# Loading four units of V with two queues, 64 partitions each

## The chip, the cores and the metric

The kernel runs on one core of a Trainium2 chip. The metric is the device time of one execution in microseconds (us). Before the change it is 344.48 us, the median of 3 runs (344.44 to 344.49).

## The reference

One decode step for a batch of 2: an attention block over a cached K and V of 4096 positions and 32 heads, a small ReLU network, and a sigmoid gate that mixes the two.

```python
q = (x @ wq).reshape(B, Sq, Hq, Dh).transpose(0, 2, 1, 3)      # B 2, Sq 1, D 512, Hq 32, Dh 128
scores = jnp.einsum("bhqd,bhkd->bhqk", q, k) * (Dh ** -0.5)    # k, v: 2 x 32 x 4096 x 128, bf16
p = _softmax(scores, axis=-1)
o = jnp.einsum("bhqk,bhkd->bhqd", p, v)
a = o.transpose(0, 2, 1, 3).reshape(B, Sq, Hq * Dh) @ wo
b = relu(x @ w1) @ w2                                          # Dff 1376
g = _sigmoid((x * gate_w).sum(-1, keepdims=True))
return g * a + (1 - g) * b
```

K and V are 67.1 MB each. All inputs together are read once: 145.46 MB by the page.

## The kernel before

The kernel writes out the order of every engine by hand. A small class collects each engine's operations in a list; an operation names the marks it waits for (`waits`), the DMA counters it waits for (`dwaits`) and the mark it sets (`signal`). Each engine then runs its list in that order, so an operation that waits holds back all that stand behind it on its engine.

K and V are each cut into eight units, 0 to 7. A unit is eight heads of one batch entry: 32,768 rows of 128 numbers, 8.39 MB. `unit_in` views it as 128 partitions of 64 KB each, and a DMA of a whole unit writes all 128 partitions with one run of 65,536 bytes for each. The buffer `kv` has five slots of 32 KB per partition. `region` joins the first four in pairs into two places of 64 KB per partition, so that two whole units fit.

The program has three stages.

- Start (to about 20 us): x, the gate, wq and w1 come in, q is computed.
- K (to about 192 us): for each piece of K, VectorE transposes 32 by 32 blocks (line 384) and TensorE multiplies by q (line 405, and line 197 for its helper). Then the softmax (lines 410 to 431).
- V and the end. For unit u, `spread(u)` puts its softmax weights into the tile `ptm` (two copies on GpSimd, one on VectorE, one on ScalarE, lines 433 to 444). `v_unit(u)` runs 64 matmuls on TensorE over the unit's 64 KB (line 458); its first one waits for the unit's DMA counter, and the last one sets the mark `pe_v_u`. `v_extract(u)` masks and sums the result on VectorE (lines 464 and 468). `o_gather` collects the units, `project` applies wo, and `ffn_f` and `ffn_last` apply w2.

All large loads are issued by SyncE, whose list is also their queue (`q1` in the page, queue SP): w1, wq, ten K loads (line 269), then V. Unit u of V goes into place u % 2 of `region`, so its issue waits for `pe_v_(u-2)`, the end of the unit that lay there before. Units 0, 1, 3, 4, 5 and 6 are one DMA each (line 277). Unit 2 comes in two halves of 32 KB per partition, to slots 4 and 0 (line 274), and unit 7 in two halves to slots 2 and 3 (line 280), both issued after `pe_v_5`. Behind V stand wo (lines 282 and 283) and w2 (lines 284 and 288) on the same queue. The counters `sem_v` count landed DMAs, 16 for each, one from each of the 16 DMA engines.

ScalarE issues two small DMAs at the start (lines 262 and 263) and one at the end. In the V stage it has one copy per unit (line 444), which waits for `pe_v_(u-2)`.

Of the kernel before, what the change touches and what calls it, by code (L numbers as in the profile page):

```python
# [85 lines left out]
def bass_gated_mix__gqa_block_cached__dense_activation_relu__decode_kernel(  # L86
# [67 lines left out]
    def psf(p0, p1, c0, n):  # L154
        return PSF[p0:p1, c0:c0 + n]
# [18 lines left out]
    names = ["x", "gw", "wq", "w1", "wo0", "wo1", "w2a", "w2b", "w2c", "w2d", "w2e", "w2f", "out"]  # L174
    sem = {n: nc.alloc_semaphore("sem_" + n) for n in names}
    sem_k = [nc.alloc_semaphore(f"sem_k{s}") for s in range(3)]
    sem_v = [nc.alloc_semaphore(f"sem_v{s}") for s in range(3)]

    mk = {}
# [8 lines left out]
    def adder(engine):  # L188
        def add(fn, waits=(), signal=None, dwaits=()):
            P.add(engine, fn, waits=[marker(w) for w in waits], signal=marker(signal) if signal else None, dwaits=dwaits)  # L190
        return add

    pool, dve, act, pe, sp = (adder(e) for e in ("pool", "dve", "act", "pe", "sp"))
# [12 lines left out]
    def held_at(e, out, lhsT, rhs, g):  # L206
# [9 lines left out]
         waits=["c_i16z"], signal="c_i16")  # L216
# [5 lines left out]
         waits=["c_i32z"], signal="c_i32")  # L222
# [6 lines left out]
         waits=["c_s4z"], signal="c_s4")  # L229
# [7 lines left out]
    v_rows = A_v_cache.rearrange("b h s d -> (b h s) d")  # L237

    def unit_in(rows, u):
        return rows[u * 32768:(u + 1) * 32768, :].rearrange("(p r) d -> p (r d)", p=128)  # L240

    region = kv[:, 0:4, :].rearrange("p (g s) n -> p g (s n)", g=2)
# [23 lines left out]
    for g, (u, halves) in enumerate(segments):  # L266
# [3 lines left out]
           waits=([f"kt_{last_of[g - 3]}"] if g >= 3 else ["pe_qr1"] if g == 2 else []))  # L270
    for u in range(7):
        if u == 2:
            for hf, dst, w in ((0, kv[:, 4, :], "kt_63"), (1, kv[:, 0, :], "pe_v_0")):
                sp(lambda e, hf=hf, dst=dst: e.dma_start(dst, unit_in(v_rows, 2)[:, 16384 * hf:16384 * (hf + 1)]).then_inc(sem_v[2 - 2 * hf], 16),
                   waits=[w])
            continue
        sp(lambda e, u=u: e.dma_start(region[:, u % 2, :], unit_in(v_rows, u)).then_inc(sem_v[u % 2], 16),
           waits=([f"pe_v_{u - 2}"] if u >= 2 else [f"kt_{last_of[7]}"] if u == 0 else [f"kt_{last_of[8]}"]))
    for hf in range(2):
        sp(lambda e, hf=hf: e.dma_start(kv[:, 2 + hf, :], unit_in(v_rows, 7)[:, 16384 * hf:16384 * (hf + 1)]).then_inc(sem_v[1 + hf], 16),  # L280
           waits=(["pe_v_5"] if hf == 0 else []))
# [3 lines left out]
       waits=[f"pt_7_{hq}" for hq in range(4)])  # L285
# [147 lines left out]
    def spread(u):  # L433
        src = ET.rearrange("p (k f e) -> p f k e", f=16, e=2)
        for hq in range(4):
            args = dict(out=ptm[32 * hq:32 * hq + 32, u % 2, :, hq, :].rearrange("p (f k) e -> p f k e", f=2),
                        in_=src[32 * hq:32 * hq + 32, 2 * u:2 * u + 2])
            waits = ["dve_et3", "c_ptm"] + ([f"pe_v_{u - 2}"] if u >= 2 else [])
            if hq < 2:
                pool(lambda e, args=args: e.tensor_copy(**args), waits=waits, signal=f"pt_{u}_{hq}")  # L440
            elif hq == 2:
                dve(lambda e, args=args: e.tensor_copy(**args), waits=waits, signal=f"pt_{u}_{hq}")
            else:
                act(lambda e, args=args: e.activation(func=ACT.Copy, **args), waits=waits, signal=f"pt_{u}_{hq}")  # L444

    def v_unit(u):
        rows = region[:, u % 2, :].rearrange("p (m c d) -> p m c d", c=4, d=128)
        halves = [kv[:, s, :].rearrange("p (m c d) -> p m c d", c=4, d=128) for s in (4, 0)]
        for m in range(64):
            t = m % 4  # L450
            waits, dwaits = [], []
            if m == 0:
                waits = [f"pt_{u}_{hq}" for hq in range(4)] + ([f"dve_y{u - 2}"] if u >= 2 else [])
                dwaits = [(sem_v[2], 16) if u == 2 else (sem_v[u % 2], 16 * (u // 2 + 1))]
            if u in (2, 7) and m == 32:
                dwaits = [(sem_v[0], 32) if u == 2 else (sem_v[2], 32)]
            at = halves[m // 32][:, m % 32] if u == 2 else rows[:, m]
            pe(lambda e, m=m, t=t, at=at: e.matmul(  # L458
                psf(32 * t, 32 * t + 32, V_B[u % 2] * BANK, 512), lhsT=ptm[:, u % 2, 4 * m:4 * m + 4, :, :],
                rhs=at, start=(m < 4), stop=(m >= 60), tile_position=(0, 32 * t)),  # L460
               waits=waits, dwaits=dwaits, signal=(f"pe_v_{u}" if m == 63 else None))

    def v_extract(u):
        dve(lambda e: e.tensor_tensor(out=Y.rearrange("p (c d) -> p c d", c=4),  # L464
                                      in0=psf(0, 128, V_B[u % 2] * BANK, 512).rearrange("p (c d) -> p c d", c=4),
                                      in1=maskc[:, :].unsqueeze(2).to_broadcast([128, 4, 128]), op=ALU.mult),
            waits=[f"pe_v_{u}", "dve_maskc"] + ([f"dve_x{u - 1}"] if u else []), signal=f"dve_y{u}")
        dve(lambda e: e.tensor_reduce(out=X2[:, u, :], in_=Y.rearrange("p (c d) -> p d c", c=4), axis=AX.X, op=ALU.add),  # L468
            waits=[f"dve_y{u}"], signal=f"dve_x{u}")
# [10 lines left out]
    def o_gather(b, us):  # L480
        for u in us:
            pe(lambda e, u=u, b=b: e.matmul(psf(0, 32, O_C0, 128), lhsT=selx[:, 24 - 8 * u:56 - 8 * u], rhs=X2[:, 4 * b + u, :],
                                            start=(u == 0), stop=(u == 3)),
               waits=[f"dve_x{4 * b + u}"] + (["dve_rinv", "dve_selx"] if u == 0 else []) + (["dve_O0"] if b else []),
               signal=(f"pe_O{b}" if u == 3 else None))
        if 3 not in us:
            return
        dve(lambda v, b=b: v.tensor_scalar(out=O_sb[:, b, :], in0=psf(0, 32, O_C0, 128), scalar1=rinv[:, b:b + 1],
                                           scalar2=gb[0:32, b:b + 1], op0=ALU.mult, op1=ALU.mult),
            waits=[f"pe_O{b}", "dve_rinv", "dve_g"], signal=f"dve_O{b}")  # L490
        for dq in range(4):
            pe(lambda e, dq=dq, b=b: e.matmul(psf(0, 128, R_C0 + 32 * b, 32), lhsT=s4[:, dq, :], rhs=O_sb[:, b, 32 * dq:32 * dq + 32],
                                              start=(dq == 0), stop=(dq == 3), tile_position=(0, 0)),
               waits=([f"dve_O{b}", "c_s4"] if dq == 0 else []), signal=(f"pe_R{b}" if dq == 3 else None))
        dve(lambda v, b=b: v.tensor_copy(out=oW[:, :, b], in_=psf(0, 128, R_C0 + 32 * b, 32)), waits=[f"pe_R{b}"], signal=f"dve_oW{b}")
# [49 lines left out]
    for u in range(8):  # L545
        if u < 7:
            spread(u + 1)
        v_unit(u)
        v_extract(u)
        if u == 3:  # L550
            o_gather(0, [0, 1, 2])
        if u == 4:
            o_gather(0, [3])
# [46 lines left out]
```

## Time and profile before

| what | value |
|---|---|
| median of the runs | 344.48 us |
| the profiled execution's own time | 344.46 us |
| its span, first to last instruction | 343.2 us |
| mean granted TensorE clock | 0.806 |
| DMA rate over the span | 424 GB/s |
| TensorE matmul busy | 200.1 us (58%) |
| VectorE busy | 176.6 us (51%) |
| ScalarE busy | 22.8 us (7%) |
| GpSimd busy | 19.6 us (6%) |

The span leaves out 1.26 us of the execution's time before the first and after the last instruction. In the view of stretches, "(x)" counts instructions, PEclk is the granted TensorE clock and the DMA share is that of the core's 16 DMA engines. In the views of slices, a digit is the busy share in tenths, at most 9.

Where the trace lists each DMA packet, a run of 65,536 bytes into one partition is one packet; there are 1,536 of them, and 1,152 of 32,768 bytes.

When V's loads are issued and when TensorE starts on the unit, by the timeline:

| load | issued at, us | first matmul on it, us | unit's last matmul releases others at, us |
|---|---|---|---|
| unit 2, first half | 189.50 | 221.20 | |
| unit 2, second half | 209.24 | 230.81 | 234.46 |
| unit 3 | 216.78 | 250.27 | 256.64 |
| unit 4 | 234.46 | 269.61 | 274.85 |
| unit 5 | 256.64 | 288.98 | 294.77 |
| unit 6 | 274.85 | 308.31 | |
| unit 7, first half | 294.77 | 318.03 | |
| unit 7, second half | 295.1 | 327.65 | |

### The profile page before, as it was taken

The page shows a single profiled execution, that of the slowest core. Times are in us where ns is not written, and L with a number is a line of the kernel's source. Part 1 is how long each engine was busy: PE and PEld are TensorE (multiplying, and loading weights), DVE is VectorE, ACT ScalarE, POOL GpSimd, SP SyncE. Part 2 cuts the span into 40 slices and gives each one's busy share as a digit, 9 for nine tenths or more (in the row PEclk, how much of TensorE's full clock was granted, in tenths as well). Part 3 has the DMA queues.
Part 4 walks back from the last instruction along what each step waited for, and adds up shares of the span by engine and source line. Part 5 has one row for each costly group of instructions (what it writes and reads, how often), then busy time and mean ns, then how long its engine had stood idle before and what let it go on. Part 6 is the DMA issues. An engine that isn't in the chain of part 4 may idle for free.

```text
span 343.2 us, 2528 instructions
## 1 busy us (share of the span) xinstructions
PE 200.1 (58%) x1226; PEld 53.4 (16%) x970; DVE 176.6 (51%) x124; ACT 22.8 (7%) x70; POOL 19.6 (6%) x34
## 2 busy tenths in 40 slices
PE   0167429799969799699799337423080503306455
PEld 0141001111111111111111012200030201102121
DVE  2239059899789899698999562202001030201021
ACT  1040000000000000000000240000000000000000
POOL 8000000000000000000000041101000010100000
PEclk9985858999989999989999856865558575856568
DMA  8998989899998999998999989999999999899996
GB/s 348 428 489 369 481 374 481 378 477 428 422 489 367 429 443 466 392 466 382 475 428 428 468 382 424 441 466 413 443 413 445 435 420 474 384 420 443 428 400 236
DMA packets 4340, 145.61 MB, mean 424 GB/s; under 512 B 485, under 2 KB 1002, under 8 KB 1258
## 3 DMA queue, kind: packets, MB, share of 16 engines
q1 hardware_dynamic: 4322, 145.46, 98.5%
q8 instruction: 8, 0.13, 0.2%
q14 instruction: 2, 0.02, 0.0%
q10 hardware_dynamic: 8, 0.00, 0.0%
HBM read 145.46 MB, written 0.00 MB: 424 GB/s over the span
## 4 chain that ended last, share of the span: by engine, by line
DMA 67%; DVE 19%; PE 11%; ACT 1%; issue 1%; POOL 0%; SPq 0%; DVEq 0%
DMA kv<-in_A_k_cache_dram 31%; DMA kv<-in_A_v_cache_dram 19%; DVE kt L384 16%; DMA kt<-in_B_w_dram 12%; PE PS L458 7%; DMA kv<-in_A_wq_dram 4%; ACT kt L426 1%; PE PS L405 1%; PE PS L197 1%; PE PS L331 1%; DVE mpad L411 1%; DVE kt L468 1%; POOL ptm L440 0%; DVE qbuf L464 0%; DVE kt L430 0%
## 5 line engine op out<-in xcount | busy, mean ns | idle before, releaser
L384 DVE STREAM_TRANSPOSE kt<-kv 128x2048 f32<-128x2048 f32 x64 | 141.2, 2274 | 22.7 <-DMA kv<-in_A_k_cache_dram 22.7
L405 PE MATMUL PS<-kt,qbuf 128*128 128x512 bf16 x256 | 107.0, 418 | 30.4 <-DVE kt L384 25.3
L197 PE MATMUL PS<-kt,qbuf 128*128 128x512 bf16 x256 | 106.5, 416 | 0.0
L458 PE MATMUL PS<-kv,ptm 128*32 128x512 bf16 x512 | 48.7, 559 | 77.3 <-DMA kv<-in_A_v_cache_dram 73.8
L464 DVE TENSOR_TENSOR qbuf<-PS,maskc 128x512 f32<-128x512 f32 x8 | 5.5, 692 | 111.4 <-PE PS L458 111.4
L405 PEld LDWEIGHTS PS<-kt,qbuf 128*128 128x128 bf16 x256 | 25.8, 101 | 139.9 <-issue 71.4
L458 PEld LDWEIGHTS PS<-kv,ptm 128*32 128x32 bf16 x512 | 18.7, 131 | 106.0 <-issue 85.4
L440 POOL COPY ptm<-kt 32x512 bf16<-32x512 bf16 x16 | 11.2, 697 | 259.2 <-DVE rsum L472 175.9
L358 ACT ACTIVATE qbuf<-PS 32x8 bf16<-32x8 bf16 x40 | 7.8, 196 | 134.3 <-PE PS L197 133.0
L444 ACT ACTIVATE ptm<-kt 32x512 bf16<-32x512 bf16 x8 | 5.1, 653 | 90.0 <-PE PS L458 88.7
L468 DVE TENSOR_REDUCE kt<-qbuf 128x128 f32<-128x512 f32 x8 | 8.2, 1029 | 0.3
L426 ACT ACTIVATE kt<-PS,negm 128x512 bf16<-128x512 f32 x8 | 5.4, 697 | 30.4 <-DVE negm L422 30.4
L331 PE MATMUL PS<-kv,xTw 128*32 128x512 bf16 x32 | 3.6, 631 | 5.9 <-DMA kv<-in_A_wq_dram 5.9
L475 PE MATMUL PS<-rsum,sell 128*32 128x1 f32 x4 | 0.4, 197 | 10.1 <-DVE rsum L472 10.1
L430 DVE STREAM_TRANSPOSE kt<-kt 128x1024 bf16<-128x1024 bf16 x4 | 5.0, 1245 | 1.7 <-ACT kt L426 1.4
L346 DVE CAST qrow<-PS 128x256 bf16<-128x256 f32 x2 | 2.4, 1397 | 6.4 <-PE PS L331 6.4
L298 PE MATMUL PS<-ident,x_sb 3*128 3x3 bf16 x4 | 0.3, 166 | 6.2 <-DMA x_sb<-in_gate_w_dram 6.2
L504 PE MATMUL PS<-kv,oW 128*2 128x512 bf16 x32 | 3.2, 570 | 0.9 <-DMA kv<-in_A_wo_dram 0.9
L566 ACT ACTIVATE out_sb<-PS 2x128 bf16<-2x128 f32 x2 | 0.5, 270 | 45.8 <-PE PS L208 45.7
L301 DVE COPY xT<-PS 128x12 bf16<-128x12 bf16 x1 | 0.2, 169 | 6.5 <-PE PS L298 6.5
L230 POOL MEMSET ptm<- 128x4096 bf16 x1 | 3.5, 3502 | 0.0
L411 DVE TENSOR_REDUCE mpad<-PS 128x1 f32<-128x2048 f32 x1 | 2.3, 2293 | 2.2 <-PE PS L197 2.2
(64 smaller groups left out, 44.2 us busy)
## 6 DMA issues: line engine op xcount, KB each, us to landing
kv<-in_A_k_cache_dram SPq DMA_DIRECT2D x4, 4096.0 KB, 31.6
kv<-in_A_v_cache_dram SPq DMA_DIRECT2D x4, 4096.0 KB, 27.3
kv<-in_A_wq_dram SPq DMA_DIRECT2D x1, 4096.0 KB, 15.0
kv<-in_A_wo_dram SPq DMA_DIRECT2D x1, 3072.0 KB, 39.3
kt<-in_B_w_dram SPq DMA_DIRECT2D x1, 1376.0 KB, 5.8
kv<-in_A_wo_dram SPq DMA_DIRECT2D x1, 1024.0 KB, 41.3
kt<-in_B_w_dram SPq DMA_DIRECT2D x1, 640.0 KB, 42.0
kt<-in_B_w_dram SPq DMA_DIRECT2D x1, 384.0 KB, 42.4
```

Of the source, the lines that this page charges most:

```text
L197: return e.add_instruction(mybir.InstMatmult(start_tensor_calc=start, stop_tensor_calc=stop, tile_size=(128, 128), tile_position=(0, 0), l ...
L331: pe(lambda e, n=n, t=t: e.matmul(psf(32 * (n % 4), 32 * (n % 4) + 32, (QR_B + n // 4) * BANK, 512), lhsT=xTw[:, t, :], rhs=wq_sb[:, t, n ...
L358: act(lambda a, hq=hq: a.activation(out=qbuf[32 * hq:32 * hq + 32, g % 2, :, :, 32 + 32 * hq], in_=cols[32 * hq:32 * hq + 32, u4 // 2, 2 * ...
L384: dve(lambda v: v.transpose(out=dst, in_=pairs[:, h, 64 * rr:64 * rr + 64]), waits=([f"pe_sc_{i - NKT}"] if i >= NKT else ["pe_h"] if i == ...
L405: return e.matmul(args[0], lhsT=args[1], rhs=args[2], start=first, stop=last)
L411: dve(lambda v: v.tensor_reduce(out=mpad[:, 0:1], in_=psf(0, 128, 0, 2048), axis=AX.X, op=ALU.max), waits=["pe_sc_63", "c_mpad"], signal=" ...
L426: act(lambda a, bk=bk, e2=e2: a.activation(out=blocks[:, bk, :, 16 * e2:16 * e2 + 16], in_=psf(0, 128, bk * BANK, 512).rearrange("p (r n) ...
L440: pool(lambda e, args=args: e.tensor_copy(**args), waits=waits, signal=f"pt_{u}_{hq}")
L444: act(lambda e, args=args: e.activation(func=ACT.Copy, **args), waits=waits, signal=f"pt_{u}_{hq}")
L458: pe(lambda e, m=m, t=t, at=at: e.matmul(psf(32 * t, 32 * t + 32, V_B[u % 2] * BANK, 512), lhsT=ptm[:, u % 2, 4 * m:4 * m + 4, :, :], rhs= ...
L464: dve(lambda e: e.tensor_tensor(out=Y.rearrange("p (c d) -> p c d", c=4), in0=psf(0, 128, V_B[u % 2] * BANK, 512).rearrange("p (c d) -> p ...
L468: dve(lambda e: e.tensor_reduce(out=X2[:, u, :], in_=Y.rearrange("p (c d) -> p d c", c=4), axis=AX.X, op=ALU.add), waits=[f"dve_y{u}"], si ...
```

## The change

Units 3, 4, 5 and 6 of V are no longer one DMA of 128 partitions on SyncE's queue. SyncE's DMA now covers partitions 0 to 63 of the unit; a second DMA, issued by ScalarE on its own queue, covers partitions 64 to 127. Both wait for the same mark, `pe_v_(u-2)`. ScalarE's DMA has a counter of its own (`sem_va`), and the unit's first matmul waits for both counters. In ScalarE's list the DMA stands ahead of its copy for `spread`, which waits for the same mark. Units 0, 1, 2 and 7, wo and w2 are loaded as before.

```diff
+    sem_va = [nc.alloc_semaphore(f"sem_va{s}") for s in range(2)]
+    SPLIT = (3, 4, 5, 6)
...
-        sp(lambda e, u=u: e.dma_start(region[:, u % 2, :], unit_in(v_rows, u)).then_inc(sem_v[u % 2], 16),
+        top = 64 if u in SPLIT else 128
+        sp(lambda e, u=u, top=top: e.dma_start(region[0:top, u % 2, :], unit_in(v_rows, u)[0:top, :]).then_inc(sem_v[u % 2], 16),
            waits=([f"pe_v_{u - 2}"] if u >= 2 else [f"kt_{last_of[7]}"] if u == 0 else [f"kt_{last_of[8]}"]))
...
                 dwaits = [(sem_v[2], 16) if u == 2 else (sem_v[u % 2], 16 * (u // 2 + 1))]
+                if u in SPLIT:
+                    dwaits.append((sem_va[u % 2], 16 * (u // 2 - (1 if u % 2 == 0 else 0))))
...
         v_unit(u)
+        if u + 2 in SPLIT:
+
+            act(lambda e, u=u: e.dma_start(region[64:128, u % 2, :], unit_in(v_rows, u + 2)[64:128, :]).then_inc(sem_va[u % 2], 16),
+                waits=[f"pe_v_{u}"])
         v_extract(u)
```

## The prediction

> **What bounds the kernel now.** I read the page first: its slices, its queue table, the chain that ended last, and the group that costs the V stage.
>
> ```profile
> DMA  8998989899998999998999989999999999899996
> q1 hardware_dynamic: 4322, 145.46, 98.5%
> DMA 67%; DVE 19%; PE 11%; ACT 1%; issue 1%; POOL 0%; SPq 0%; DVEq 0%
> L458 PE MATMUL PS<-kv,ptm 128*32 128x512 bf16 x512 | 48.7, 559 | 77.3 <-DMA kv<-in_A_v_cache_dram 73.8
> ```
>
> One queue moves all that matters, its packets fill 98.5% of the 16 DMA engines' span, and the V matmuls idle longer (77.3 us) than they work (48.7). The reader is to see that nothing but transfer time counts here. Next the chain of waits in order of time (start us, us, what), for the V stage:
>
> ```profile
> 216.78 33.35 DMA kv<-in_A_v_cache_dram
> 250.13 0.14 issue
> 250.27 6.35 PE PS L458 x63
> 256.62 0.02 issue
> 256.64 32.21 DMA kv<-in_A_v_cache_dram
> 288.84 0.14 issue
> ...
> 297.88 42.44 DMA kt<-in_B_w_dram
> ```
>
> Unit 3 lands at 250.13, unit 5 at 288.84: two units, 16.78 MB, in 38.71 us, so 19.36 us a unit and 433 GB/s. A DMA is issued 32 to 33 us before it lands and needs 19.36, so some 13 us of earlier transfers are always queued ahead of it: an issue that is late by less costs nothing. Then the stretches:
>
> ```profile
> core 0: us, PE busy (x) PEld busy (x) DVE busy (x) ACT busy (x) POOL busy (x), PEclk, DMA share, GB/s
> 217.00:250.00 33.00, 6.85 (x64) 2.33 (x64) 4.02 (x6) 1.11 (x2) 2.37 (x4) 0.62 1.01 434
> 250.00:289.00 39.00, 12.64 (x144) 5.84 (x147) 4.71 (x8) 1.31 (x2) 2.57 (x4) 0.68 1.00 434
> ```
>
> The DMA share is 1.00: no gap is left between packets for a second queue to fill. A unit puts 128 rows on 16 engines, eight packets each, so a packet takes 19.36 / 8 = 2.42 us, and the packet records say the same (65,536 bytes: median 2.42 us; 32,768 bytes: 1.21). That is 27.1 bytes per ns and engine, the same in K and V. Last, the DMA slices from 250 to 262.1 us, each 0.30 us:
>
> ```profile
> DMA  9950409099504090994050909940459099504090
> GB/s 433 1517 217 0 217 0 1083 0 433 1517 217 0 217 0 1083 0 433 1517 217 0 217 0 1083 0 433 1354 217 0 217 217 1083 0 433 1300 217 0 217 0 1300 0
> ```
>
> Bytes are booked when packets start: every eight slices (2.42 us) about ten engines start within 0.6 us, and five more 1.8 us after the first. The engines run in step, in two bunches. This decides below.
>
> **The change, part by part.** *Issues.* SP keeps four DMAs with half the rows; ScalarE gets four more. Bytes and 65,536-byte packets stay the same; the 64 further completion marks at 9 ns each make 0.04 us over 16 engines. A ScalarE issue took 0.23 us, a V issue of SP 0.33. Behind it on ScalarE waits only the copy for `spread`, released by the same mark:
>
> ```profile
> 234.46 0.66 ACT L444 ACTIVATE ptm<-kt 32x512 bf16<-32x512 bf16 x1 [17.02 <-PE PS L458]
> 256.64 0.66 ACT L444 ACTIVATE ptm<-kt 32x512 bf16<-32x512 bf16 x1 [21.52 <-PE PS L458]
> ```
>
> It moves back 0.3 us; its reader is the next unit but one, over 30 us later. Cost nothing; without that cover 4 x 0.33 = 1.3 us. *The wait added* on the first matmul of units 3 to 6 holds back that unit's 64 matmuls and the next issue; with both halves landed it is one more check (the chain shows 0.14 us from landing to matmul), inside the 13 us of queue. Cost nothing.
>
> *Order.* ScalarE's half no longer stands behind unit 2 on SP: from 216.78 the engines alternate between the queues, packet by packet as I assume. This alone delays unit 2 and loses no transfer time while a queue is full (worked out under the rivals).
>
> *Pace of a 64-partition transfer.* The trace has none. From above, an engine keeps 27.1 bytes per ns wherever it writes: half a unit takes 4 x 2.42 = 9.68 us, no cost. From below, the rate belongs to the way into the partitions: 64 partitions have half the ways, two engines share one, and half a unit alone takes 19.36 us. The nearest rows, all on 128 partitions, show the same rate to a fraction of a per cent in every packet: a fixed-width way filled to the brim, with no spare for a second engine. I take the lower end. [...]
>
> With both halves in flight, the lower half's ways and the upper's could work at once, if the two engines of a shared way were on opposite halves. Started in step, both write a lower row, then both an upper one: each packet takes 4.84 us while the other eight ways stand empty, and nothing pulls them apart, as both finish together. With ten of 16 engines in the early bunch, at least two of eight pairs are in step, however they are paired, and a unit has landed only when its last pair has. So:
>
> 1. 216.78: 11.5 packets of unit 2 are left on SP (to 230.76 at 1.21 each). Unit 3's four upper packets alternate with them: 4 x (1.21 + 4.84) = 24.2, to 241.0. The other 7.5 of unit 2: 9.1, so it lands at 250.1, not 230.76.
> 2. Its last 32 matmuls take 3.65 (230.81 to 234.46): unit 4 is issued at 253.8. Unit 3's lower half, alone on SP, has done 3.7 / 4.84 = 0.8 packets; 3.2 alternate with unit 4's upper: 3.2 x 9.68 = 31.0. Unit 3 lands at 284.8, unit 5 is issued 6.4 later (291.2).
> 3. Both queues stay full: unit 4 lands 38.7 later (323.5), unit 6 is issued at 328.9, unit 5 lands at 362.2.
> 4. Unit 6's upper half has 0.8 packets left (7.7, to 369.9), then 3.2 lower ones alone: 15.5, so it lands at 385.4, not 308.15.
>
> Check: 32 packets per engine at 2.42 more each are 77.4 us. Behind unit 6 the 35 us to the end are as before. The execution profiled took 344.46 (span 343.2 plus 1.26; the median of the runs is 344.48): 344.46 + 77.4 = 421.9. A pair that is apart by d saves d on each packet with both halves in flight, some 2 x (3.2 + 4 + 4 + 0.8) = 24. In the first bunch I take 0.12 us for the tightest pair: 2.9 less, **419 us**.
>
> **The rivals.** *A, the pairs come apart* (33%). If pairs work on opposite halves, or an engine mixes both queues finely, each packet takes 2.42 while both queues hold halves. Step 1 stays (unit 2 writes all ways, unit 3's upper half crowds half of them). Then unit 3 lands at 269.3 and unit 5 is issued at 275.7; unit 4's upper half ran out at 273.2, so SP is alone for 2.5 us; unit 4 lands at 288.8, unit 5 at 308.2, and 2.7 lower packets of unit 6 run alone at 4.84 to 327.6: 19.4 late, 364 us. If even step 1 runs at 3.63 a round, 9.7 less: 354. For it: the second bunch shows that engines drift. Against it: the slices keep their pattern over 12 us. Anything between 354 and 410 belongs here.
>
> *B, not slower: the rate is the engine's* (13%). Only the order changes. Unit 2 lands 9.68 late (240.4), unit 4 is issued at 244.1, when unit 3 still has transfers until 250.1: 6 us of cover. Further on, unit 5 is issued at 262.6 with work until 269.5, unit 6 at 281.0 until 288.8, unit 7 at 300.9 until 308.2. The engines never run dry: 344.5 us. For it: an engine's rate is as constant as a way's. It also holds if each half went to eight engines of its own, since every engine then has the packets it has now. It would cost from the point where the cover falls under zero, and 6 us is the least.
>
> *C, faster* (7%). The 1.00 share leaves nothing in the stretch; what is left is the spread of the engines, 1.9 us from the first to the last completion mark of unit 3. Were the load to be levelled by the second queue, at most 1.9 us: 342.6. Against it: each engine keeps as many rows.
>
> **How the numbers follow.** In step (410 to 426) 47%, A 33%, B 13%, C 7%. The forecast is that of the likeliest, 419. From 354 (A's least) to 426 (in step with nothing saved, and 4 us for crowding worse than by halves) hold 80%. A measurement of this kernel can tell about 0.2% (0.7 us) from no change: slower 0.80, same 0.13, faster 0.07.
>
> **What would show it.** In the changed profile, 65,536-byte packets of units 3 to 6 that take about 4.8 us, and DMA rates of 217 GB/s from 254 us on with a DMA share still near 1; unit 2's second half landing near 250, unit 6's near 385; the rest from there 35 us. Packets of 2.4 us between 254 and 315 mean A or, with unit 6 at 308, B. The forecast is wrong if a stretch with one half alone runs above 400 GB/s.

## The result, and the profile after

The changed kernel takes 434.26 us, the median of 4 runs (432.2 to 439.35), against 344.49 us beside it: ratio 1.2585, 95% interval 1.2567 to 1.2604. The ratio is that of the three fast runs; the fourth, 439.35 us, counts as slow. That is slower, as forecast, but by 15 us more than forecast, and 8 us above the range of 354 to 426 us. The profiled execution took 432.2 us, 87.7 more than the profiled one of before (344.46).

The page of the changed kernel:

```profile
DMA  8999999999899999999999999999999999999971
GB/s 353 420 430 481 395 435 441 481 397 468 384 432 456 403 426 451 456 421 450 395 324 198 173 304 201 237 286 208 213 274 249 219 280 213 213 221 347 418 319 43
q1 hardware_dynamic: 4066, 128.68, 80.1%
q10 hardware_dynamic: 328, 16.78, 16.9%
L463 PE MATMUL PS<-kv,ptm 128*32 128x512 bf16 x512 | 43.4, 509 | 170.7 <-DMA kv<-in_A_v_cache_dram 169.6
```

The DMA engines are as busy as before, and from the 21st slice to the 36th (215 to 388 us) they move about half as much. `q10` is ScalarE's queue; it carries 16.78 MB, the four upper halves. The V matmuls, now line 463, wait 170.7 us instead of 77.3. By stretches, cut where units 2 to 6 land:

```profile
core 0: us, PE busy (x) PEld busy (x) DVE busy (x) ACT busy (x) POOL busy (x), PEclk, DMA share, GB/s
217.00:260.00 43.00, 3.77 (x36) 1.37 (x40) 0.29 (x1) 0.00 (x0) 0.00 (x0) 0.57 1.06 248
260.00:287.00 27.00, 3.31 (x32) 0.95 (x24) 2.12 (x3) 0.66 (x1) 1.28 (x2) 0.50 0.98 233
287.00:326.00 39.00, 6.36 (x70) 3.02 (x70) 2.11 (x3) 0.66 (x1) 1.28 (x2) 0.59 1.00 239
326.00:363.00 37.00, 5.50 (x70) 2.53 (x70) 2.60 (x5) 0.66 (x1) 1.28 (x2) 0.59 0.99 236
363.00:396.00 33.00, 5.40 (x64) 2.28 (x64) 2.12 (x3) 0.66 (x1) 1.28 (x2) 0.60 0.96 246
```

A DMA share near 1.00 beside 233 to 248 GB/s instead of 434: the engines are not idle, each packet takes longer (the 512 of the split units a mean of 4.59 us, before the change 2.42). The chain of waits has four long waits of this kind in the V stage, up to 363 us (start us, us, what; the first two):

```profile
230.39 29.28 another core or an unknown queue
...
263.31 23.73 another core or an unknown queue
```

The view does not name the loads. By their completion marks they are SyncE's own: the second half of unit 2 (last mark at 259.67 us) and the lower halves of units 3, 4 and 5 (287.05, 326.00 and 362.80). The upper halves of these units had landed at 252.96, 307.94 and 344.61, so it is always the lower half that comes last.

### The profile page after: what moved, and what is told of

Read it like the earlier page. It is cut to its first block, busy times and chain, and to the rows that moved or that the text cites. A ratio compares the mean times of both kernels' runs of the same rounds, so it can differ in the third digit from the quotient of the medians.

```text
span 430.9 us, 2533 instructions
## 1 busy us (share of the span) xinstructions
PE 194.5 (45%) x1226; PEld 52.5 (12%) x970; DVE 176.4 (41%) x124; ACT 22.9 (5%) x70; POOL 19.6 (5%) x34
## 3 DMA queue, kind: packets, MB, share of 16 engines
q10 hardware_dynamic: 328, 16.78, 16.9%
## 4 chain that ended last, share of the span: by engine, by line
DMA 49%; another core or an unknown queue 27%; PE 13%; DVE 8%; SPq 2%; issue 0%; DVEq 0%
DMA kv<-in_A_k_cache_dram 25%; DMA kt<-in_B_w_dram 12%; DMA kv<-in_A_v_cache_dram 9%; DVE kt L387 8%; PE PS L463 5%; DMA kv<-in_A_wq_dram 3%; PE PS L408 3%; PE PS L199 3%; SPq L283 1%; PE PS L334 1%; SPq L285 1%; DVE kt L473 0%; DVE qbuf L469 0%; PE PS L487 0%
## 5 line engine op out<-in xcount | busy, mean ns | idle before, releaser
L463 PE MATMUL PS<-kv,ptm 128*32 128x512 bf16 x512 | 43.4, 509 | 170.7 <-DMA kv<-in_A_v_cache_dram 169.6
L463 PEld LDWEIGHTS PS<-kv,ptm 128*32 128x32 bf16 x512 | 17.3, 122 | 195.3 <-issue 151.1
L487 PE MATMUL PS<-kt,selx 128*32 128x128 f32 x16 | 3.3, 344 | 0.6 <-DVE kt L473 0.6
L445 DVE COPY ptm<-kt 32x512 bf16<-32x512 bf16 x8 | 3.1, 387 | 0.2
```

What stands on the lines that cost most here:

```text
L463: pe(lambda e, m=m, t=t, at=at: e.matmul(psf(32 * t, 32 * t + 32, V_B[u % 2] * BANK, 512), lhsT=ptm[:, u % 2, 4 * m:4 * m + 4, :, :], rhs= ...
```

## The experiments

Two theories stood at the start. W: the transfer rate belongs to the ways into the partitions; the 64 partitions of the lower or of the upper half have half of them, so two engines share one. Q: two queues that take turns on an engine are what costs. "Way" is the author's supposition: no trace names one, and what the runs can show is the time of a packet by the partitions it goes to. All diffs are against the changed kernel, or against the kernel that is named. In the three kernels with other cuts (32 to 95, sixteens, 28 to 91) SyncE issues every piece and ScalarE none; their diffs show the pieces only.

### One queue, the same cut

```diff
+        if u in SPLIT:
+            sp(lambda e, u=u: e.dma_start(region[64:128, u % 2, :], unit_in(v_rows, u)[64:128, :]).then_inc(sem_va[u % 2], 16))
...
-            act(lambda e, u=u: e.dma_start(region[64:128, u % 2, :], ...
```

> Units 3 to 6 are still cut at partition 64, but both halves are issued by SyncE on one queue, the upper behind the lower; ScalarE issues nothing. Theory W (the rate belongs to the ways into the partitions, and 64 adjacent partitions have half of them): every packet of these units is shared by two engines at all times, 4.84 to 5.12 us each (the changed kernel's lone halves took 5.12), so 32 packets x 2.42 to 2.70 more: 422 to 431 us, DMA rate near 205 to 217 GB/s in the stretch, engines less spread at the end than in the changed kernel. Rival Q (two queues taking turns on an engine are what costs): one queue, no turns, packets of 2.42 us, 344.5 us.

430.43 us (before: 344.40). The stretches from unit 2's landing to unit 4's:

```profile
232.00:273.00 41.00, 3.60 (x32) 1.08 (x32) 2.10 (x3) 0.66 (x1) 1.27 (x2) 0.50 0.99 205
273.00:313.00 40.00, 7.20 (x70) 3.29 (x70) 2.10 (x3) 0.66 (x1) 1.28 (x2) 0.54 1.01 210
```

There are no turns here, and the loss is nearly the same: Q falls. The 65,536-byte packets have a median of 5.12 us, 6% over twice 2.42, and the last engine ends some 2 us behind the first, about as before the change (1.8).

### Two queues, cut along the rows

```diff
-        top = 64 if u in SPLIT else 128
-        sp(... region[0:top, u % 2, :], unit_in(v_rows, u)[0:top, :] ...
+        end = 16384 if u in SPLIT else 32768
+        sp(... region[:, u % 2, 0:end], unit_in(v_rows, u)[:, 0:end] ...
...
-            act(... region[64:128, u % 2, :], unit_in(v_rows, u + 2)[64:128, :] ...
+            act(... region[:, u % 2, 16384:32768], unit_in(v_rows, u + 2)[:, 16384:32768] ...
```

> Units 3 to 6 are loaded by both queues at the same moments as in the changed kernel, but cut along the row: SyncE loads the first 32 KB of all 128 partitions, ScalarE the second 32 KB. Theory W: each engine keeps its own way, packets of 32,768 bytes at 1.21 us, only the order changes as in rival B of the prediction: 344.5 us, at most 1 us apart. Rival Q (two queues taking turns): 64 packets per engine take turns, as slow as the changed kernel, 420 to 435 us.

344.71 us against 344.40: ratio 1.0008, interval 0.9999 to 1.0018, no difference that can be told. Its queues and stretches:

```profile
q1 hardware_dynamic: 4322, 128.68, 87.2%
q10 hardware_dynamic: 584, 16.78, 11.4%
...
217.00:250.00 33.00, 7.21 (x64) 2.36 (x64) 2.18 (x4) 0.66 (x1) 1.28 (x2) 0.61 1.00 430
250.00:289.00 39.00, 12.69 (x140) 5.85 (x140) 4.71 (x8) 1.32 (x2) 2.56 (x4) 0.68 1.00 431
```

The same 16.78 MB on ScalarE's queue at the same moments cost nothing and gain nothing. Unit 2's second half lands at 240.2 us here; rival B of the prediction had worked out 240.4 for a change of order alone.

### Other partitions: 32 to 95, then the two ends

```diff
+        lo, hi = (32, 96) if u in SPLIT else (0, 128)
+        sp(... region[lo:hi, u % 2, :], unit_in(v_rows, u)[lo:hi, :] ... sem_v ...)
+        if u in SPLIT:
+            for lo in (0, 96):
+                sp(... region[lo:lo + 32, u % 2, :], unit_in(v_rows, u)[lo:lo + 32, :] ... sem_va ...)
```

> One queue (SyncE). Units 3 to 6 are cut in three: partitions 32 to 95 in one DMA, then 0 to 31, then 96 to 127. Theory W, in the form that 0 to 63 have one set of eight ways and 64 to 127 the other, with 32 partitions reaching as many ways as 64: the middle piece reaches all 16 ways and runs at 2.42 us a packet (4 packets, 9.7 us), each outer piece has eight ways, 2 packets per engine at 4.84 to 5.12 (9.7 to 10.2 us each): a unit takes 29.0 to 30.2 us, 4 x 9.7 to 10.8 more, 383 to 388 us. Rival H (any transfer of 64 or fewer partitions is slow, whichever they are): 422 to 431 us.

391.77 us, 4 over the expected band. Two stretches in which the middle piece runs, each followed by one with the ends:

```profile
231.00:240.00 9.00, 3.24 (x32) 0.94 (x24) 2.12 (x3) 0.66 (x1) 1.27 (x2) 0.50 1.11 371
243.00:262.00 19.00, 0.00 (x0) 0.00 (x0) 0.00 (x0) 0.00 (x0) 0.00 (x0) 0.50 0.92 207
262.00:272.00 10.00, 6.25 (x70) 3.01 (x70) 2.11 (x3) 0.66 (x1) 1.28 (x2) 0.77 1.08 382
274.00:293.00 19.00, 0.00 (x0) 0.00 (x0) 0.00 (x0) 0.00 (x0) 0.00 (x0) 0.50 0.98 221
```

The middle piece has 64 partitions too, and its packets take 2.42 us, the full pace (the stretch also holds the first slow packets of the ends). The ends take 4.8 to 5.1. So it is not the number of partitions but which they are: "any 64 partitions are slow" falls. Partitions 32 to 95 take packets at the pace of all 128 (2.42 us), 0 to 63 at half of it (5.12 with one queue), and the ends, 0 to 31 and then 96 to 127, at about the pace of 0 to 63 (4.8 to 5.1).

### Sixteen partitions, and one shared way

```diff
-    SPLIT = (3, 4, 5, 6)
+    SPLIT = (3,)
...
+        cuts = [(0, 16), (16, 32), ...] if u in SPLIT else [(0, 128)]
+        for n, (lo, hi) in enumerate(cuts):
+            sp(... region[lo:hi, u % 2, :], unit_in(v_rows, u)[lo:hi, :] ... sem_va if n else sem_v ...)
```

> One queue (SyncE), only unit 3 is cut, into eight pieces of 16 adjacent partitions, one row per engine. Theory W (the ways belong to the partitions, four engines share one here): packets of 9.7 to 10.3 us, unit 3 takes 78 to 82 us instead of 19.4: 403 to 407 us. Rival F (a transfer that does not keep each engine on its own partitions runs at half pace, whatever the number that share): packets of 4.85 to 5.1, 364 to 367 us.

395.51 us (before: 344.48); unit 3 costs 51.0 more. From 240 to 280 us:

```profile
240.00:280.00 40.00, 0.00 (x0) 0.00 (x0) 1.64 (x3) 0.18 (x1) 0.83 (x2) 0.54 0.99 128
```

The time is 7.5 us under the expected band. Packets take 8.1 us, not 9.7 (the engines are some 6 us apart, so two neighbouring pieces are under way together, which is probably why), but far over the 5.1 of a fixed half pace, which falls. Packets into 16 adjacent partitions (8.1 us) are slower than packets into 64 (5.12).

The second kernel cuts unit 3 at other places. Its first piece is 32 to 95, which ran at 2.42 us a packet, moved down by four rows. If each engine has four adjacent rows, this moves one engine's rows, and by theory W two of the 16 engines may then share a way:

```diff
+        cuts = [(28, 92), (0, 28), (92, 128)] if u in SPLIT else [(0, 128)]
```

> One queue, only unit 3 is cut: first partitions 28 to 91, then 0 to 27, then 92 to 127. [...] Theory W alone: 2 of 16 engines at 4.8 to 5.1 us a packet, 14 at 2.42. Theory W with coupling (a crowded way holds back engines that write elsewhere): 2 at 4.8 to 5.1, the other 14 clearly over 2.42, about 3.0 by what unit 7's packets showed beside two late engines in the changed kernel (1.52 us instead of 1.21). The time, with the odd pieces behind it, 360 to 385 us, tells nothing.

377.29 us. The packets of the first piece that start from 232.7 to 236.8 us, from the packet records (start: duration):

```
232.75: 2.65  232.82: 2.63  232.83: 2.62  232.98: 2.61  233.03: 2.61  233.12: 5.05  233.31: 5.05
233.41: 2.57  233.78: 2.54  233.91: 2.53  234.23: 2.52  234.69: 2.50  234.79: 2.50  234.91: 2.49
235.04: 2.49  235.20: 2.48  ...  236.44: 2.45  236.75: 2.44
```

Two packets at 5.05 and all others on their way from 2.65 to 2.42, as theory W has it if two engines share one way. So two engines can halve each other's pace, and in this stretch that does not hold back the other 14. (At its start, beside the end of unit 2, this piece's packets took 4.3; those of the piece 32 to 95 took 2.42 there. The runs do not show why.)

### One and two units split

```diff
-    SPLIT = (3, 4, 5, 6)
+    SPLIT = (3,)
```

> Only unit 3 is split over the two queues, units 4 to 6 are loaded whole by SyncE. Theory W: the upper half alternates with unit 2 (unit 2 lands near 259.7 as in the changed kernel), then the lower half alone at 5.1 us a packet; 8 packets per engine at 2.4 to 3.2 more, unit 2's packets some 4 us more: 364 to 372 us. If the engines that fall behind in the changed kernel do so once and not with every unit, the completion marks at the end are as far apart as there (12 us); if with every unit, some 3 us. Rival Q: the halves meet only while ScalarE's queue is busy, afterwards packets of 2.42: 355 to 360 us.

375.59 us (before: 344.40), above the band: the first split unit costs 31.2 us, and the completion marks at the end are 3.4 us apart; with two units split, below, they are 3.2, so the spread does not simply grow with the number of units. The packets of unit 2 that run beside the upper half took 2.35 us and more (median 2.5), none the 1.21 that by theory W half of them should have kept, and the upper ones 4.2 to 6.3 (median 5.2).

```diff
-    SPLIT = (3, 4, 5, 6)
+    SPLIT = (6,)
...
-                    dwaits.append((sem_va[u % 2], 16 * (u // 2 - (1 if u % 2 == 0 else 0))))
+                    dwaits.append((sem_va[u % 2], 16))
```

> Only unit 6 is split over the two queues. Theory W with crowding: as with unit 3 alone (375.6), the upper half runs beside the rest of a whole unit, here unit 5 in packets of 65,536 bytes, and the lower half alone or beside unit 7: 24 us for unit 6's eight packets per engine, 5 to 8 for the crowded whole units, 1 to 4 for the spread: 374 to 381 us. Rival: a lone last unit is cheaper as less stands behind it, 362 to 368 us.

379.90 us: inside the band; a last unit is no cheaper.

```diff
-    SPLIT = (3, 4, 5, 6)
+    SPLIT = (3, 4)
```

> Units 3 and 4 are split over the two queues, 5 and 6 loaded whole by SyncE. Theory W with crowding: the crowding of a whole unit is paid once; the second unit adds only its own packets while both queues hold halves (mean 4.3 us, from the changed kernel's 69.6 us of extra packet time per engine less unit 3's 24.3, over three units: 15.1) and 1 to 4 us of spread: 391 to 395 us. Rival (each split unit costs what unit 3 alone costs, 31 us): 406 us.

396.09 us: the second unit adds 20.5 us, 1 over the band and far from another 31. What unit 3 pays beside a whole unit is paid once.

### Unit 3's upper half waits for unit 2

```diff
-                waits=[f"pe_v_{u}"])
+                waits=[f"pe_v_{u}"], dwaits=([(sem_v[0], 32)] if u == 1 else []))
```

> The changed kernel, but ScalarE's upper half of unit 3 waits until all of unit 2 has landed (one more counter wait on that one DMA), so that no half runs beside a whole unit at the start; units 4 to 6 as changed. Theory W with crowding: unit 2 lands at 231 as before the change and its packets stay at 1.21 us (6.3 us less per engine), unit 3's halves start together at 231, packets of 4.2 to 4.9 us: 32 x 1.8 to 2.5 more, unit 7 crowded by late engines (2 to 4), engines spread by 2 to 9: 408 to 430 us, likeliest 420. Rival O (what costs beyond the halved pace is not the overtaking of unit 2): 430 to 436 us.

426.73 us, between the two: the crowding of units 2 and 7 falls from 10.2 to 2.6 us and the spread at the end from 11.6 to 2.4, but the packets of the split units rise from a mean of 4.59 to 4.91. Once both queues had work, no packet took less than 4.67. The engines go from lower to upper rows and back in one rhythm, but in two bunches: at 267.5 us eight write lower and eight upper rows, and these packets too take 4.8 us and more.

### Nudges: engines moved against each other

Were it only that partners write the same half at the same moment, one more turn for some engines should help. The base is the kernel just above. A tiny load that nobody reads is added to SyncE's queue ahead of unit 4's lower half, on eight engines, on all 16, or twice on eight:

```diff
+        if u == 4:
+            for i in range(1):
+                sp(lambda e, i=i: e.dma_start(nudge[8 * i:8 * (i + 1), :], unit_in(v_rows, 0)[8 * i:8 * (i + 1), 0:256]).then_inc(sem_n, 16),
+                   waits=["pe_v_2"])
```

> The kernel in which unit 3's upper half waits for unit 2 (426.7 us, its engines write lower halves all together, then upper halves all together), with one tiny load added: eight rows of 512 bytes into a small tile that nobody reads, on SyncE's queue between unit 3's and unit 4's lower half. It gives eight of the 16 engines one more turn on SyncE's queue. Theory W, in step: if each of these eight shares its way with one of the other eight, the turn puts them on the upper half while the partners are on the lower one, from about 265 us on; packets fall from 4.85 towards 2.42 while both queues hold halves, up to 26 packets of 2.4 us less: 362 to 400 us. If the eight share among themselves, or if being in step is not what costs: 422 to 430 us.

> The same with a tiny load of 16 rows, one for each engine: every engine gets the turn, so no engine is moved against its partner. Theory W, in step: as without it, 422 to 430 us. If a tiny load itself changes something (any nudge helps): as with eight rows.

> The same with two tiny loads of eight rows, one behind the other: the eight engines get two more turns and are again on the same half as their partners. Theory W, in step, if one tiny load is one turn: 415 to 430 us. If its row and its completion mark are turns of their own, one load would already be two turns, and this one four: both this and the single one at 415 to 430 us.

426.63, 424.07 and 426.43 us: 2.7 us below the base at most, far from a gain of 27 or more. In the first of them an engine's tiny row starts at 262.57 us and its completion mark at 267.66, with an upper packet between: two turns, an even number, so this test could not tell. An odd number, with two runs in each of 8, 3 or 4 rows:

```diff
-    nudge = sb("nudge", [128, 256], dt.bfloat16)
+    nudge = sb("nudge", [8, 2, 512], dt.bfloat16)
...
+    e.dma_start(nudge[:, :, 0:256], unit_in(v_rows, 0)[0:8, 0:1024].rearrange("p (a b) -> p a b", a=2)[:, :, 0:256])
```

> As with one tiny load of eight rows, but two separate runs of 512 bytes in each row. The trace of the single tiny load showed its row and its completion mark taking a turn each, with an upper packet between them, so eight engines got two turns and stayed on the same half; two runs and a mark are three turns, an odd number. Theory W, in step: these eight engines then write the upper half while their partners write the lower one, packets fall from 4.85 towards 2.42 us from about 275 us on while both queues hold halves: some 20 packets, 2.4 us each at most: 370 to 405 us. If the eight share their ways among themselves, or if being in step is not what costs: 422 to 430 us, packets of 4.8 us.

> The odd nudge with three rows: three engines get three more turns on SyncE's queue. Whichever engines share a way, at least one of the three has its partner outside. Theory W, in step: from about 275 us on each pair that was taken apart writes different halves, so two or six engines show packets well under 4.6 us while both queues hold halves, the others stay at 4.85; the time stays at 420 to 430 us, as a unit waits for its slowest engine. Rival G (the halved pace belongs to a larger group than two engines, or to any mix of halves): all packets stay at 4.7 to 5.1.

> The odd nudge with four rows, four engines. Theory W, in step: eight engines show short packets if each of the four has its partner outside, none if the four are two pairs; the time 415 to 430 us. Rival G: none, all packets 4.7 to 5.1.

426.62, 427.16 and 427.43 us. In the one with three rows, packets by start and duration (U upper, the rest lower):

```
284.72 U 4.85   285.27 4.84   285.96 4.86   286.09 4.86   286.12 4.85   286.17 4.86   286.21 4.85
287.67 4.86   287.73 4.84   287.77 4.84   287.90 U 4.86   288.09 4.86   288.20 4.86   288.21 U 4.86
288.25 4.85   288.56 4.86
```

Three engines are on the other half than the 13, as wanted, and gain nothing. In the one with eight rows, the packets under way at 285 us:

```
280.82 4.84   280.96 U 4.85   281.05 U 4.85   281.08 U 4.85   281.16 U 4.84   281.64 4.84   282.60 4.86   282.82 U 4.85
282.85 U 4.85   282.97 U 4.86   283.00 U 4.86   283.28 4.86   283.36 4.85   283.56 4.84   283.80 4.85   283.87 4.86
```

Followed back from each packet's start to the end of the one before it, the eight lower ones belong to the eight engines that had a nudge row. So eight engines are on the other half than the other eight, and no packet that starts from 280.8 to 292 us takes less than 4.83. All this is as rival G had it. The last nudge stands ahead of unit 3, both halves held until unit 2 has landed:

```diff
-        if u == 4:
+        if u == 3:
...
-                   waits=["pe_v_2"])
+                   waits=["pe_v_1"], dwaits=[(sem_v[0], 32)])
```

> The odd nudge on eight engines, now ahead of unit 3's lower half, with both halves of unit 3 starting after unit 2 has landed. In the earlier nudges the turn of the upper half's completion mark fell between the nudge's turns on some engines, so not all eight were moved. Theory W, in step, each of the eight with its partner outside: during the first packets (233 to 250 us) most packets are well under 4.6 us, down to 2.4; later marks bring pairs together again, so the time falls only in part, 395 to 424 us. Rival G (any mix of halves runs at half pace): all packets 4.7 to 5.1, 424 to 432 us.

431.19 us. The tiny rows were over before ScalarE's half arrived, so nobody was moved, but the run shows the step in its purest form, in slices of 0.61 us from 241.8 to 266 us:

```profile
DMA  9900000099000000995000009950000099900000
GB/s 975 758 0 0 0 0 0 0 758 975 0 0 0 0 0 0 542 1083 108 0 0 0 0 0 325 1300 108 0 0 0 0 0 217 1300 217 0 0 0 0 0
```

All 16 engines start a packet within 1.0 us, then none for 4: one round of 16 lower rows, one of 16 upper rows, 4.95 us each. Twice 2.42 is 4.84, so even this costs little more than two packets of before, one behind the other.

### The sum over the packets

For each kernel, the time of the 65,536-byte packets that start after 214 us over 2.42 each, and of the 32,768-byte ones over 1.213, summed and divided by 16 engines; then how far the last completion mark of w2 lies behind the mean, less the 0.8 us of before. Figures in us.

| kernel | 65,536 bytes | 32,768 bytes | last engine | sum | measured |
|---|---|---|---|---|---|
| changed kernel | 69.6 | 10.2 | 8.4 | 88.2 | 87.7 |
| one queue | 84.0 | 2.1 | 0.2 | 86.3 | 86.0 |
| upper half waits for unit 2 | 79.6 | 2.6 | 0.4 | 82.6 | 82.3 |
| units 3 and 4 | 44.5 | 6.3 | 1.1 | 51.9 | 51.7 |
| unit 6 | 31.1 | 2.6 | 2.0 | 35.7 | 35.5 |
| unit 3 | 24.3 | 5.9 | 1.2 | 31.4 | 31.2 |
| middle and ends | 46.6 | 1.3 | -0.1 | 47.8 | 47.4 |

In these seven kernels the sum meets the measured loss within 0.5 us: the whole loss is packet time and the wait for the last engine. Nothing that can be told is matmul, issue or semaphore.

## Why the prediction was wrong, and where it was right

The bound was read rightly: with a DMA share of 1.00 a second queue has nothing to fill, and the column cut shows it (344.71 against 344.40 us). The issues and the added wait cost nothing, as said, though a ScalarE issue took 0.50 to 0.55 us and not 0.23, and moved the copy back by 0.6:

```profile
215.10 0.55 ACTq L556 DMA_DIRECT2D kv<-in_A_v_cache_dram  x1
215.70 0.66 ACT L447 ACTIVATE ptm<-kt 32x512 bf16<-32x512 bf16 x1 [6.75 <-PE PS L463]
```

The pace of a 64-partition transfer was rightly taken from the lower end. Its size was a little off: 5.12 us where one half follows the other on one queue, not 4.84. The ways behind it, and that 64 partitions have half of them, no run shows; the runs show packet times by partitions: 5.12 us for 0 to 63 and 64 to 127 on one queue, 2.42 for 32 to 95, 4.8 to 5.1 for 0 to 31 and 96 to 127, 8.1 for 16 adjacent ones. The constant rate from which the prediction took a way without spare is that of 1,530 of the 1,536 packets of 65,536 bytes before the change (2.42 to 2.43 us); six took 2.89 to 2.97. Two halves at once can be compared with one behind the other by the DMA rates: 207 GB/s with one queue (240 to 390 us), 216 in the kernel whose upper half waits for unit 2 (250 to 375 us), 4% more, and 239 in the changed kernel (260 to 396 us), some 15% more, there paid back by the crowding and the spread.

The steps against the chain, first matmul after landing:

| unit landed | forecast | measured |
|---|---|---|
| 2, second half | 250.1 | 259.7 |
| 3 | 284.8 | 287.3 |
| 4 | 323.5 | 326.2 |
| 5 | 362.2 | 363.1 |
| 6 | 385.4 | 396.4 |

Three terms missed, of which two nearly cancel.

- Step 1, "4 x (1.21 + 4.84)": the packets of unit 2 were to keep 1.21. Beside the upper half, from 224 to 248 us, they took 2.5 to 3.1 (median 2.7), and the upper ones 4.4 to 5.8. Unit 2 was 9.6 us later than forecast.
- Steps 2 and 3, where "nothing pulls them apart": in this execution something did. Packets that start from 275 to 285 us, some engines on each half, took 3.0 to 4.8 us (median 3.7), a part of rival A, and the mean of all 512 was 4.59. This won back 8.7 of the 9.6 us by unit 5. It was luck: with units 3 and 4 split, which has the same loads in the same order up to 290 us, the packets from 275 to 290 us took 4.83 to 5.12. The overtaking in step 1 alone therefore does not do it, and the cause stays open.
- Step 4, "so it lands at 385.4": 14 of unit 6's 16 lower marks had come by 384.8 us. The last two came at 394.9 and 396.2, since two engines had fallen behind, and their last rows met unit 7's packets of the engines that had gone on: 7.4 and 7.8 us a packet. This is the step that failed. The forecast let all engines end together, and the upper end of the range held 4 us for crowding. Crowding (6.3 of it in unit 2, the rest in unit 7) and spread were 10.2 and 8.4.

In the terms of the sum: the split packets were to cost 74.5 us (77.4 less 2.9) and cost 69.6; the packets of whole units and the wait for the last engine were put at nothing and cost 18.6 together. With the upper half of unit 3 held back until unit 2 had landed these two fell to 3.0, so in this trace they go with the overtaking. They need not: with unit 3 alone split, or units 3 and 4, unit 2 is overtaken too, the crowding is 5.9 and 6.3, but the wait for the last engine only 1.2 and 1.1.

Behind unit 6, the 35 us to the end were 34.5 (396.4 to the span's 430.9).

The rivals: B fell with one queue and with the middle piece, C with the column cut. A happened in part and in the middle only.

The picture of partners in step was not borne out. That two engines can halve each other's pace while the others keep theirs is shown for one queue, by the cut at 28 to 91 (two packets of 5.05 us, the others down to 2.44). For two queues the forecast made the same 4.84 us out of partners that write the same half at the same moment, and the figure came out (means of 4.83 to 4.99 in the kernels without overtaking) by luck, for engines on opposite halves kept it too: three against 13, and eight against eight. With three, at least one has its partner outside. With eight, all might have had their partners among themselves: the trace does not name the engines. One possible reason is that many crowded ways hold back the engines on free ones as well, which the packets of unit 2 beside the upper half suggest (2.5 at the least, where by theory W half of them had free ways); with one crowded way nothing of it was seen from 234 to 238 us. But then the 3.0 to 3.7 us of some packets in the changed kernel need a reason too. What sets the pace with two queues stays open.

## What to carry to other kernels

Read the DMA share in the stretch before adding a queue: at 1.00 a second queue brought only a change of order here (344.71 against 344.40 us). If a large load must be cut in two, cut it along the rows and keep all 128 partitions in each piece; that was free here (and gained nothing), while the cut at partition 64 cost 22 us a unit on average. If only 64 partitions are wanted, 32 to 95 ran at twice the pace of 0 to 63 (2.42 against 5.12 us a packet).

## What the runs showed of the hardware that was not expected

- Packets into 64 partitions of one half took 5.12 us on one queue, 6% more than twice 2.42. Packets into 16 adjacent partitions took 8.1 us, 16% less than four times 2.42, with the engines some 6 us apart. By theory W two engines share a way in the first case, four in the second.
- While two late engines wrote their last rows, the others were slower: from 386 to 394 us in the changed kernel, the 32,768-byte packets of unit 7 took 1.51 us (median of 69) instead of 1.21. With two slow engines in unit 3 (the cut at 28 to 91, packets of 5.05 us) the others came down to 2.44. The difference was not explained. One engine of unit 7 took 3.9 us a packet; its rate and those of the two late ones (7.4 and 7.8 us for 65,536 bytes) add up to 25.6 bytes per ns, just what two engines reach together at 5.12 us a packet. An estimate from these figures, by theory W, is that the three shared one way.
- The queues take turns run by run. One 65,536-byte row is a turn: with the nudge ahead of unit 3, 16 engines write a lower row and then an upper one, five rounds of 16 packets in 24.2 us, three of SyncE's queue and two of ScalarE's. A 4-byte completion mark is one too: with the first nudge the mark follows its tiny row by 5.09 us, with an upper packet between.
- Order is fragile: in the one trace of each, the kernel in which unit 3 overtakes unit 2 has split packets that are 10 us cheaper in all, and crowding and a spread that are 15.6 us dearer (10.2 and 8.4 against 2.6 and 0.4). The same overtaking with units 3 and 4 split did not make the packets cheaper.
